# A gated recurrence with a maxout layer on one core: column quarters, a four-step weight conversion, one joined sum, and a new order of all work

## The chip, the cores and the metric

The kernel runs on one core of a Trainium2 chip. A core has a matrix engine (PE), a vector engine (DVE), an activation engine (ACT), a general engine (POOL) and a sequencer for transfers (SP); each works through its own queue in order, and semaphores make one wait for another. The metric is device time in microseconds; the time of a kernel is the median of its runs.

## What is computed

The first half is a recurrence with a complex gate per channel; the second is a three-way maxout layer on its output. The four weight matrices arrive as 64-bit floats, everything else as 32-bit.

```python
batch, n_heads, seq, head_dim = 4, 8, 768, 48       # x: 3072 tokens, 384 wide; d_ff 768
mag = np.sqrt(a_re * a_re + a_im * a_im)
scale = np.minimum(mag, 0.999) / (mag + 1e-06)
a = (a_re + 1j * a_im) * scale
for t in range(S):
    S_ = a[:, :, t, :, None] * S_ + k[:, :, t, :, None] * v[:, :, t, None, :]
    y[:, :, t] = np.einsum('bhd,bhde->bhe', q[:, :, t], S_.real)
x = y.transpose(0, 2, 1, 3).reshape(B * S, H * D)
h = np.maximum(np.maximum(x @ w1, x @ w2), x @ w3)
out = h @ w_out
```

(The reference keeps real and imaginary parts of the state apart; the lines are shortened here.)

## The kernel before

**Tiling.** Tokens are worked in 12 groups; a group is one stretch of 128 positions of two sequences, its two chunks named x and y. Six groups after one another belong to one pair of sequences and hand on a state.

**Order.** The order of all work is written out by hand in one string, `SCHEDULE`: some 1,900 words such as `csx:3`, a step, a chunk and a group. `program` runs them in turn, and each word issues its instructions at the end of its engine's queue (`Bound` chains the instructions of an engine in that order). Transfers go into SP's queue, accumulating transfers into POOL's. `SLOTS` says, for each matrix result in turn, which of four pairs of PSUM banks it gets. `OTHER` is a set of words whose step goes to DVE in place of ACT or POOL: `copy`, `magnitude`, `increase` and a few branches ask `other()`.

**Steps of a group**, in the order in which the data passes them:

- loads `Lr`, `Li` (gates), `Lk`, `Lq`, `Lv`; a load of k, q or v is four transfers (`load_kq`, `load_v`);
- gates, `sqr` to `turn` (function `gates`): the logarithm of the magnitude goes to the tile Ln, the angle in turns to w. Ln, Exp, Sin and Arctan run on ACT; Ln and Exp live in one activation table, Sin and Arctan in another, and `activation` issues a table load when the set changes. `relu`, `abs`, `Lnop` and `addw` are the steps that may change engines;
- angles: `cs` sums the turns along time with a triangular matrix on PE, `t` and `nf` take off whole turns, `af`, `sa` and `sb` give cosine and sine, `Cd` carries the last angle to the next group by an accumulating transfer;
- turns: `sums`, `En`, `Ek`, `Eq`, `F`, `f0` to `f3` (decay factors), `mk`, `mq`, `uk`, `uq`, `kEn` (DVE products), `tpk`, `tpq` (transposes on PE), `Kc`, `Qc` (copies out of PSUM);
- factors and scores: `Q1`, `Q2`, `KB`, `QB`, `QG` on DVE, `A` and `B` on PE, `g0` to `g3` and `b0`, `b1` pick the results;
- state: `dk` on PE, `h0` to `h3` on DVE; output of the recurrence: `y` on PE, `x` copies it out;
- the layer: `U01` to `U12` are up products of nine 128x128x256 matmuls each, `u01` to `u12` the relu and the maxima. The down product is a scheme of seven products: `S1` to `S4` on DVE, `P1` to `P7`, `Px`, `Py` on PE, and `r1`, `r6`, `r5`, `r7`, `r57`, `ox`, `oy` add the parts into the output tile `ot`; `D` stores it. Group 0 uses a plain form (`U01x` and so on, `O`, `o`) while the weights are not yet there.

**Weights.** Twelve blocks are loaded raw (`WL0` to `WL11`, 768 KB each) and converted from 64 to 32 bits by integer steps on the two words of a number: `Wa` on ACT (absolute value of the high word, scaled), then `Wb` (clamp), `Wc` (shift), `We` (merge the low word's top bits) and `Wf` (merge the sign) on DVE. `Wg` subtracts one weight block from another, `T`, `t`, `M` and `m` build a product of w1 and w_out, `J1` to `J4` the seven products' factors.

**Buffers.** Some tiles are fixed (`const`), others come from pools with one or two buffers under a tag; chunk tiles such as `t`, `nf`, `CS`, `K` and `Q` rotate through two. Ek and Eq share a tag.

Of the kernel before, what the change touches and what calls it, by code (L numbers as in the profile page):

```python
# [26 lines left out]
turn1:0 Lry:1 sqr:1 t1:0 WL11:0 Lkx:0 tx:0 nfx:0 Wa11:0 Wb10:0 csy:0 afx:0 sax:0 mkx:0 Wb11:0 Wc10:0 Lix:1 sbx:0
uqx:0 sqi:1 Lix:2 Wc11:0 Lky:0 tpqx:0 ty:0 add:1 f3x:0 f2x:0 ukx:0 Fy:0 Qcx:0 We10:0 Wf10:0 nfy:0 tpkx:0 We11:0
lnL:1 WL2:0 Q2x:0 kEnx:0 Eqy:0 expe:1 Eky:0 relu:1 xor:1 expw:1 QBx:0 Kcx:0 abs:1 T2:0 T0:0 t0:0 CL:0 KBx:0 WL1:0
Wa1:0 pw:1 Q1x:0 mky:0 Wb1:0 f0y:0 f1y:0 Wc1:0 t2:0 f2y:0 Wf11:0 lne:1 Lnop:1 Ax:0 g0x:0 Lry:2 g1x:0 We1:0 g2x:0  # L30
half:1 Lqy:0 Cdx:0 f3y:0 Liy:2 Lvx:0 mqy:0 Wa2:0 Wb2:0 lnw:1 expL:1 M0:0 mulw:1 Wc2:0 M1:0 mulai:1 dkx:0 Wf1:0
stt:1 afy:0 say:0 sby:0 Wg1:0 sqi:2 WL4:0 Wa4:0 g3x:0 sumsx:1 Lrx:2 Cdy:0 sqr:2 M2:0 We2:0 QGx:0 atan:1 Wb4:0 Wf2:0
Lvy:0 Eqx:1 Enx:1 Ekx:1 uky:0 Zg:0 tpky:0 h1x:0 m0:0 m1:0 Lkx:2 Z3:0 Wg2:0 Wc4:0 uqy:0 tpqy:0 Lqx:1 Kcy:0 Qcy:0
Bx:0 b0x:0 turn:1 b1x:0 h2x:0 mqx:1 Fx:1 f0x:1 We4:0 f1x:1 Wf4:0 f2x:1 add:2 csx:1 tx:1 yx:0 KBy:0 Q2y:0 nfx:1 xx:0
h3x:0 f3x:1 lnL:2 expe:2 Q1y:0 WL5:0 Wa5:0 Lkx:1 sumsy:1 csy:1 Eky:1 ty:1 Ay:0 kEny:0 Wb5:0 WL7:0 relu:2 mkx:1
g0y:0 Wc5:0 expw:2 U01x:0 nfy:1 abs:2 u01x:0 Lvy:1 We5:0 Eqy:1 Z2:0 g1y:0 Wa7:0 QBy:0 afy:1 Wf5:0 Eny:1 g2y:0 g3y:0
Wb7:0 Wg4:0 U11x:0 xor:2 By:0 dky:0 U02x:0 Lvx:1 b1y:0 h1y:0 b0y:0 QGy:0 yy:0 addw:2 lnw:2 expL:2 xy:0 U11y:0 Wg5:0
u02x:0 U02y:0 afx:1 half:2 u11x:0 Wc7:0 lne:2 We7:0 mulw:2 mulai:2 sbx:1 h2y:0 Z4:0 sax:1 h3y:0 stt:2 atan:2 Wf7:0
U12x:0 u12x:0 say:1 sby:1 Cdy:1 WL8:0 Cdx:1 turn:2 ukx:1 uqx:1 U01y:0 u01y:0 u11y:0 Wa8:0 U12y:0 csy:2 ty:2 u12y:0
csx:2 tpqx:1 tx:2 u02y:0 Qcx:1 nfy:2 Lnop:2 nfx:2 tpkx:1 Fy:1 kEnx:1 Wb8:0 Wc8:0 We8:0 Kcx:1 Wg7:0 Wf8:0 U21y:0  # L40
Wg8:0 KBx:1 f0y:1 u21y:0 Lky:1 Lqy:1 mky:1 afy:2 sumsx:2 dkx:1 Q1x:1 f1y:1 f2y:1 f3y:1 Enx:2 U21x:0 u21x:0 afx:2
U22y:0 u22y:0 Oy:0 Lqx:2 mqy:1 uky:1 uqy:1 tpqy:1 Ekx:2 Lix:3 Q2x:1 say:2 sby:2 sbx:2 sax:2 Eqx:2 h0x:1 h1x:1 QGx:1
h2x:1 oy:0 QBx:1 mkx:2 h3x:1 Qcy:1 Q1y:1 tpky:1 Kcy:1 Ax:1 g0x:1 Q2y:1 Liy:3 sqi:3 Fx:2 sumsy:2 g1x:1 g2x:1 U22x:0
Lrx:3 u22x:0 g3x:1 f3x:2 f2x:2 f1x:2 f0x:2 Lry:3 sqr:3 add:3 lnL:3 expe:3 Ay:1 relu:3 J3:0 g0y:1 g1y:1 mqx:2 g2y:1
Bx:1 KBy:1 kEny:1 lne:3 Ox:0 Eky:2 b1x:1 Eny:2 QBy:1 b0x:1 h0y:1 ukx:2 By:1 Eqy:2 yx:1 g3y:1 xx:1 b1y:1 Lqy:2 mqy:2
Lvx:2 ox:0 Lky:2 mky:2 b0y:1 tpkx:2 expw:3 Kcx:2 uqx:2 Lnop:3 uqy:2 tpqx:2 Qcx:2 QGy:1 dky:1 h1y:1 kEnx:2 sumsx:3
uky:2 Ekx:3 h2y:1 Eqx:3 Enx:3 yy:1 xy:1 Fy:2 f3y:2 h3y:1 dkx:2 f2y:2 abs:3 KBx:2 h0x:2 h1x:2 Q1x:2 f0y:2 f1y:2
U11:1 u11:1 tpky:2 Kcy:2 Lky:3 QBx:2 QGx:2 addw:3 Lqx:3 h2x:2 mqx:3 h3x:2 xor:3 half:3 Cdx:2 tpqy:2 Qcy:2 Q2x:2
lnw:3 kEny:2 expL:3 sumsy:3 Eqy:3 Q2y:2 Eny:3 Lkx:3 mkx:3 Fx:3 Eky:3 U01:1 Ax:2 Q1y:2 J1:0 mulw:3 mulai:3 g0x:2
g1x:2 u01:1 Cdy:2 f3x:3 f2x:3 g2x:2 g3x:2 J2:0 Bx:2 f0x:3 Dx:0 f1x:3 Dy:0 stt:3 KBy:2 h0x:3 U12:1 b0x:2 b1x:2 u12:1  # L50
S3:1 Lvy:2 yx:2 U02:1 QBy:2 Lvx:3 Lry:4 atan:3 turn:3 Liy:4 csy:3 csx:3 Lix:4 Lrx:4 sqr:4 sqi:4 add:4 lnL:4 ty:3
xx:2 By:2 u02:1 Ay:2 S1:1 nfy:3 relu:4 tx:3 expe:4 S2:1 expw:4 P5:1 P6:1 g0y:2 afy:3 say:3 sby:3 nfx:3 sbx:3 g1y:2
afx:3 sax:3 abs:4 dky:2 P1:1 Lqy:3 g2y:2 g3y:2 b1y:2 J4:0 QGy:2 P7:1 Px:1 P2:1 b0y:2 h0y:2 h1y:2 ukx:3 tpkx:3 lne:4
Lnop:4 r1:1 Liy:5 mky:3 h2y:2 h3y:2 S4:1 Kcx:3 uqx:3 yy:2 Lqx:4 kEnx:3 mqy:3 tpqx:3 Qcx:3 P3:1 r6:1 xy:2 Py:1 r5:1
r7:1 P4:1 Fy:3 uky:3 r57:1 f0y:3 f1y:3 xor:4 half:4 oy:1 ox:1 Q1x:3 addw:4 dkx:3 h1x:3 Lvy:3 f2y:3 f3y:3 h0y:3
h2x:3 sumsx:4 Ekx:4 h3x:3 lnw:4 QGx:3 expL:4 Eqx:4 Fx:4 KBx:3 U11:2 Dx:1 QBx:3 mulai:4 Q2x:3 f2x:4 Enx:4 u11:2
# [986 lines left out]
```

## Time and profile before

| what | us |
|---|---|
| runs | 557.14, 561.46, 561.69 |
| median | 561.46 |
| span of the profiled execution | 556.9 |
| the same: PE / DVE / ACT / POOL busy | 524.6 / 490.4 / 370.0 / 74.4 |
| time in activation table loads (45) | 57.7 |
| time in the 792 matmul records of the up products | 177.4 |

The span runs from the first to the last instruction of one execution. Busy time is the union of an engine's instructions; for PE their ends are modelled, so a busy PE is not yet one at its peak. One matmul in 32-bit floats is two records. Nearly every instruction carries line 210, the helper that records all of them, so groups are told apart by the names of the tiles they write and read: `xhx<-xhx,up` is the running maximum, `ot<-ot,op` the joining of the down product, `xhx<-xhx` and `w<-w,xhx` weight steps, `g<-g,f` the state's decay.

### The profile page before, as it was taken

To read this page: it belongs to the slowest core of one execution; us is meant where nothing else is said; L and a number is where in the kernel's file an instruction comes from. 1 tells how busy PE (TensorE), PEld (TensorE's weight loads), DVE (VectorE), ACT (ScalarE), POOL (GpSimd) and SP (SyncE) were. 2 spreads that over 40 slices of the span, in tenths; PEclk is the share of its full clock that TensorE was granted. 3 is DMA by queue.
4 is the path that set the end of the run, shared out by engine and by line. 5 is a ranking of instruction groups with operands and counts; after the bars stand their busy time and mean duration, and the time that the engine had idled before them with its cause. 6 is when DMAs were issued, how large, how long until landed. Compare 5 with 4: busy or idle time off the path is not lost.

```text
span 556.9 us, 22739 instructions
## 1 busy us (share of the span) xinstructions
PE 524.6 (94%) x10086; PEld 449.0 (81%) x10086; DVE 490.4 (88%) x770; ACT 370.0 (66%) x652; POOL 74.4 (13%) x117
## 2 busy tenths in 40 slices
PE   1669799989999999999999999999999999999997
PEld 0356588778888898888988888988888888998986
DVE  5999999989998899999988897999999999886524
ACT  5999989867965867787766858777646855530100
POOL 8105250002030001000120200120010020000000
PEclk9869999999999999999999999999999999999999
DMA  8977976456055164235364136542361144000000
GB/s 218 287 191 156 206 154 102 78 105 123 18 108 109 21 123 77 48 63 92 68 115 82 33 61 121 110 88 50 58 126 31 32 88 82 10 31 2 7 25 29
DMA packets 142530, 49.09 MB, mean 88 GB/s; under 512 B 130528, under 2 KB 135648, under 8 KB 142432
## 3 DMA queue, kind: packets, MB, share of 16 engines
q1 hardware_dynamic: 136272, 37.77, 31.9%
q0 software_dynamic: 6160, 9.87, 10.4%
q8 instruction: 79, 1.29, 1.0%
q14 instruction: 19, 0.16, 0.1%
HBM read 33.03 MB, written 4.72 MB: 68 GB/s over the span
## 4 chain that ended last, share of the span: by engine, by line
PE 84%; DVE 6%; DMA 4%; SPq 2%; issue 1%; ACT 1%; POOL 0%; DVEq 0%
PE up L210 34%; PE op L210 24%; PE y L210 7%; PE A L210 5%; PE tp L210 4%; PE dk L210 4%; PE sums L210 3%; PE cs L210 2%; SPq L210 2%; DMA xhx<-in_moe_w_out_dram 2%; PE F L210 2%; DVE xhx L210 1%; PE B L210 1%; DMA k<-in_k_dram 1%; DMA ar<-nf 1%
## 5 line engine op out<-in xcount | busy, mean ns | idle before, releaser
L210 PE MATMUL up<-xhx,w 128*128 128x256 f32 x792 | 177.4, 382 | 0.1
L210 PEld LDWEIGHTS up<-xhx,w 128*128 128x128 f32 x792 | 148.6, 190 | 21.5 <-PE B L210 0.3
L210 ACT ACT_TABLE_LOAD x45 | 57.7, 1283 | 1.5 <-PEq L1027 0.8
L210 ACT COPY atm<-B 32x128 f32<-32x128 f32 x96 | 24.5, 255 | 36.9 <-DVE atm L210 22.9
L210 PE MATMUL op<-wo,xhx 128*128 128x192 f32 (+1 forms) x220 | 48.5, 364 | 0.0
L210 DVE TENSOR_TENSOR Q<-Q,f 112x1024 f32<-112x1024 f32 (+1 forms) x48 | 45.4, 950 | 0.8 <-ACT Q L210 0.6
L210 ACT ACTIVATE f<-F 48x232 f32<-48x232 f32 x96 | 34.4, 359 | 13.2 <-PE F L210 5.4
L210 POOL DMA_DIRECT2D ar<-nf x40 | 34.2, 1280 | 65.3 <-DVE ar L210 54.7
L210 PE MATMUL y<-atm,vb 128*32 128x64 f32 x1152 | 39.4, 221 | 1.4 <-issue 1.1
L210 PEld LDWEIGHTS op<-wo,xhx 128*128 128x128 f32 x220 | 36.5, 190 | 4.3 <-DVE q L210 0.3
L210 POOL DMA_DIRECT2D Ln<-e x11 | 11.1, 1005 | 214.6 <-ACT e L210 53.9
L210 PE MATMUL y<-QG,g 112*32 112x64 f32 x1408 | 38.4, 219 | 0.9 <-issue 0.8
L210 PEld LDWEIGHTS y<-atm,vb 128*32 128x32 f32 x1152 | 32.5, 109 | 6.4 <-issue 3.6
L210 PEld LDWEIGHTS y<-QG,g 112*32 112x32 f32 x1408 | 34.8, 109 | 1.3 <-issue 1.0
L210 DVE TENSOR_TENSOR ot<-ot,op 128x192 f32<-128x192 f32 (+1 forms) x67 | 27.1, 413 | 9.0 <-PE op L210 4.3
L210 PE MATMUL op<-wo,strassen 128*128 128x192 f32 x176 | 33.0, 331 | 0.0
L210 PE MATMUL A<-Q,K 112*32 112x80 f32 x1536 | 31.6, 234 | 1.3 <-DVE Q L210 1.3
L210 DVE COPY_PREDICATED atm<-masko,A 128x256 f32<-128x256 uint8 x72 | 31.2, 435 | 1.6
L210 PE MATMUL op<-w,strassen 128*128 128x192 f32 x176 | 32.5, 329 | 0.0
L210 PEld LDWEIGHTS A<-Q,K 112*32 112x32 f32 x1536 | 27.2, 110 | 5.0 <-issue 1.9
L210 ACT COPY Q<-tp 112x1024 f32<-112x1024 f32 x23 | 23.3, 1013 | 10.3 <-PE tp L210 10.0
L210 ACT COPY ot<-op 128x192 f32<-128x192 f32 (+1 forms) x13 | 4.5, 342 | 38.2 <-PE op L210 38.2
(151 smaller groups left out, 1120.8 us busy)
## 6 DMA issues: line engine op xcount, KB each, us to landing
ar<-in_a_re_dram SPq DMA_DIRECT2D x24, 192.0 KB, 3.7
ai<-in_a_im_dram SPq DMA_DIRECT2D x24, 192.0 KB, 3.8
q<-in_q_dram SPq DMA_DIRECT2D x96, 48.0 KB, 2.6
k<-in_k_dram SPq DMA_DIRECT2D x96, 48.0 KB, 2.9
vb<-in_v_dram SPq DMA_DIRECT2D x96, 48.0 KB, 3.1
out_dram<-ot SPq DMA_DIRECT2D x23, 192.0 KB, 2.8
Ln<-e POOLq DMA_DIRECT2D x11, 384.0 KB, 4.7
w<-L POOLq DMA_DIRECT2D x9, 384.0 KB, 4.7
```

The costliest lines, as they stand in the source:

```text
L210: ins = f(*a, **kw)
```

## The change

Five things change together.

1. `cs` is computed in four column quarters of the PE array, 32 wide, in place of two halves of 64: eight matmuls of 192 columns in place of four.
2. The weights' conversion has four steps in place of five. `Wb` now comes first and clamps the high word from both sides, `Wa` is a Prelu with a slope that keeps the sign and the scale, `Wc` shifts, `We` merges the low word and writes the result. `Wf` is gone.
3. `r5` and `r7` become one addition, `r75`, over two neighbouring half tiles.
4. Three biases of activations are numbers in the instruction in place of a column in memory. The tiles of k, q, t, nf, CS, Ln, Ek, Eq, En, K, Q and ot are fixed pairs in place of pool tiles; Ek and Eq have their own.
5. `SCHEDULE`, `SLOTS` and `OTHER` are new from end to end. The loads stand in bundles, once a group; the words of one kind for x and y stand together more often; 52 words are in `OTHER` in place of 38.

The diff, without the three lists:

```diff
-    LAST = float(np.array(0x0FEFFFFF, dtype=np.int32).view(np.float32))
+    LAST = float(np.array(0x47EFFFFF, dtype=np.int32).view(np.float32))
...
-        if step == "a":
-            activation(out=ex.bitcast(FP), in_=high.bitcast(FP), func=AF.Abs, scale=2.0 ** -112)
-        elif step == "b":
-            dve.tensor_single_scalar(out=ex.bitcast(FP), in_=ex.bitcast(FP), scalar=LAST, op=OP.min)
+        if step == "b":
+            dve.tensor_scalar(out=ex.bitcast(FP), in0=high.bitcast(FP), scalar1=LAST, scalar2=-LAST, op0=OP.min,
+                              op1=OP.max)
+        elif step == "a":
+            activation(out=ex.bitcast(FP), in_=ex.bitcast(FP), func=AF.Prelu, alpha=-2.0 ** 32,
+                       scale=-2.0 ** -112 if i in (0, 3, 6) else 2.0 ** -112)
         elif step == "c":
-            if i in (0, 3, 6):
-                dve.tensor_scalar(out=ex, in0=ex, scalar1=3, scalar2=-0x80000000, op0=OP.logical_shift_left,
-                                  op1=OP.bitwise_or)
-            else:
-                dve.tensor_single_scalar(out=ex, in_=ex, scalar=3, op=OP.logical_shift_left)
+            dve.tensor_single_scalar(out=ex, in_=ex, scalar=3, op=OP.logical_shift_left)
         elif step == "e":
-            dve.scalar_tensor_tensor(out=ex, in0=low, scalar=29, in1=ex, op0=OP.logical_shift_right, op1=OP.bitwise_or)
-        elif step == "f":
-            dve.scalar_tensor_tensor(out=dst.bitcast(I32), in0=high, scalar=-0x80000000, in1=ex,
-                                     op0=OP.bitwise_and, op1=OP.bitwise_xor)
+            dve.scalar_tensor_tensor(out=dst.bitcast(I32), in0=low, scalar=29, in1=ex, op0=OP.logical_shift_right,
+                                     op1=OP.bitwise_or)
...
-                activation(out=e, in_=e, func=AF.Ln, scale=1e-6 * math.exp(-LNMAX), bias=least)
+                activation(out=e, in_=e, func=AF.Ln, scale=1e-6 * math.exp(-LNMAX), bias=math.exp(-LNMAX))
...
-                for j in range(2):
-                    dst, m = ps[j * L64:(j + 1) * L64, ch * HC:(ch + 1) * HC], slice(ch * L64, (ch + 1) * L64)
-                    mm(out=dst, lhsT=upto[:, m], rhs=every(T["w", g][:, c * DM:(c + 1) * DM], j), start=True, stop=True)
+                for o in (0, L64, 32, L64 + 32):
+                    j, m = o // L64, slice(ch * L64 + o % L64, ch * L64 + o % L64 + 32)
+                    mm(out=ps[o:o + 32, ch * HC:(ch + 1) * HC], lhsT=upto[:, m],
+                       rhs=every(T["w", g][:, c * DM:(c + 1) * DM], j), start=True, stop=True)
...
-            E = T[name, x] = nat2.tile([P, DM], FP, tag=name[:1 + (n == 1)], name=name[:1 + (n == 1)])
+            E = T[name, x] = es[name][c]
...
+                if name == "r75":
+                    two_ = ot.rearrange("p c n -> p (c n)")[:, NH:3 * NH].rearrange("p (u n) -> p u n", u=2)
+                    again = yl.rearrange("p (u n) -> p u n", u=1).to_broadcast([P, 2, NH])
+                    dve.tensor_tensor(out=two_, in0=again, in1=ps[:, 1, 0:DM].rearrange("p (u n) -> p u n", u=2), op=OP.add)
+                    return
```

Where the prediction speaks of the lists, it speaks of these places. Old, around `h0x:3` and `U12:1`, and new, around `Q1y:2`:

```
old: ... stt:3 KBy:2 h0x:3 U12:1 b0x:2 b1x:2 u12:1 S3:1 Lvy:2 yx:2 U02:1 QBy:2 Lvx:3 ...
new: ... atan:3 Cdx:2 Cdy:2 turn:3 h0y:2 Q2y:2 h3x:2 Q1y:2 U01:1 U02:1 sumsx:3 b0x:2 ...
```

The head of the new list, and one of its bundles of loads:

```
Lrx:0 sqr0:0 Lix:0 sqi0:0 add0:0 lnL0:0 expe0:0 expw0:0 lne0:0 relu0:0 Lnop0:0 Zf:0 CL:0 Lry:0 WL0:0 Wb0:0 Liy:0 sqr1:0
abs0:0 sqi1:0 WL3:0 Wa0:0 add1:0 xor0:0 lnL1:0 expe1:0 expw1:0 lne1:0 relu1:0 WL6:0 Wc0:0 Wb3:0 We0:0 half0:0 Lnop1:0
...
u12:4 Lix:8 Liy:8 Lkx:6 Lvx:6 Lqx:6 Dx:3 Dy:3 Lqy:6 S3:4 h1x:5 h1y:5 Q2y:5 sumsy:6 Fx:6 lnw:7 Eky:6 Eny:6 Enx:6 afx:6
```

More of the change, by code (lines that the diff above doesn't have):

```diff
@@ L27 @@
[L27 to L56, printed above, removed]
@@ L138 @@
+xx:8 abs:10 xy:8 relu:11 xy:9 Qcx:10 addw:11 Qcy:10 u01:9 xx:10 Kcy:11 Qcy:11 xx:11 u11:11
 """.split())
@@ L546, in gates @@
             else:
[L547 removed]
+                activation(out=part("Ln") if g >= ADDS else L, in_=L, func=AF.Relu, scale=-0.5, bias=LNMAX)
         elif name == "Lnop":
```

240 lines of the change are left out of this document (131 added, 109 removed).

## The prediction

> **What bounds the kernel now.** The page comes first, for the busy shares and the slices of the span.
>
> ```profile
> span 556.9 us, 22739 instructions
> PE 524.6 (94%) x10086; PEld 449.0 (81%) x10086; DVE 490.4 (88%) x770; ACT 370.0 (66%) x652; POOL 74.4 (13%) x117
> PE   1669799989999999999999999999999999999997
> DVE  5999999989998899999988897999999999886524
> ACT  5999989867965867787766858777646855530100
> ```
>
> TensorE (PE) is full from the tenth slice on; before that VectorE (DVE) is full and PE is not. Averages hide this, so the second view is busy time by stretch (columns: length, then busy time and instructions of PE, weight load, DVE, ACT, POOL; granted clock; DMA share; GB/s).
>
> ```profile
> 0.00:14.00 14.00, 1.80 (x3) 0.69 (x4) 7.47 (x19) 7.98 (x17) 11.26 (x40) 1.00 0.83 219
> 14.00:56.00 42.00, 32.83 (x353) 20.32 (x354) 41.59 (x67) 41.48 (x69) 10.73 (x18) 0.84 0.87 209
> 56.00:84.00 28.00, 23.47 (x550) 19.92 (x550) 27.86 (x43) 24.47 (x48) 11.52 (x13) 1.00 0.84 179
> 84.00:142.00 58.00, 56.25 (x1301) 45.61 (x1300) 55.82 (x86) 45.66 (x83) 5.01 (x6) 1.00 0.57 102
> 142.00:250.00 108.00, 107.03 (x2156) 93.91 (x2155) 100.36 (x158) 80.25 (x136) 10.90 (x13) 1.00 0.37 71
> 250.00:530.00 280.00, 279.86 (x5612) 247.52 (x5611) 248.13 (x388) 169.81 (x304) 24.99 (x30) 1.00 0.34 65
> ```
>
> From 14 to 84 us DVE idles 0.41 + 0.14 = 0.55 us, from 84 to 142 us another 2.18. PE idles 1.11 us from 142 to 530 us, all of it but 0.14 before 250 us. So the time is made of two pieces: DVE work up to some place in the list, then PE work from there to the end. To find the place I summed over the schedule list, word by word, DVE work so far plus PE work still to come, at the durations of the groups (the main ones are quoted below), neighbours' overlap taken off. The largest sum stands at the word h0x:3, and the timeline shows it as the first row here, with the PE block (U12:1) and the DVE maximum (u12:1) that follow it:
>
> ```profile
> 139.01 0.55 DVE L210 TENSOR_TENSOR g<-g,f 112x384 f32<-112x384 f32 x1
> 139.48 0.95 DVE L210 TENSOR_TENSOR xhx<-xhx,up 128x768 f32<-128x768 f32 x1
> 139.63 4.15 PE L210 MATMUL up<-xhx,w 128*128 128x256 f32 x18
> 553.39 0.62 DVE L210 TENSOR_TENSOR ot<-ot,op 128x192 f32<-128x192 f32 x2 [0.56 <-PE op L210]
> ```
>
> From 139.6 us PE has 413.8 us of nearly unbroken work to 553.4; the last addition and its store take the other 3.5. What happens before 139.6 us is what the change can shorten: DVE's queue, with its 6.53 us of idle in the first 14 us (14 - 7.47).
>
> The three runs were 557.14, 561.46 and 561.69 us. The profiled execution (556.9) lies 4.6 below the median, near the fastest run. I add the change of the span to 561.46.
>
> **The change, part by part.** Weights. The twelve blocks lose step f, which merged the sign. Step b (clamp) now reads the strided high words itself and keeps the sign; ACT's step a becomes Prelu; c loses a second operation; e writes the result.
>
> ```profile
> L210 DVE SCALAR_TENSOR_TENSOR w<-w,xhx 128x768 int32<-128x768 int32 x3 | 2.9, 952 | 0.0
> L210 DVE TENSOR_SCALAR xhx<-xhx 128x768 f32<-128x768 f32 x12 | 7.5, 621 | 2.8 <-ACT xhx L210 2.7
> L210 DVE TENSOR_TENSOR w<-w,L 128x768 f32<-128x768 f32 x11 | 10.5, 951 | 0.0
> L210 DVE TENSOR_SCALAR Ln<-L 128x768 f32<-128x768 f32 x4 | 2.2, 551 | 0.0
> L210 DVE TENSOR_TENSOR k<-E,k 128x384 f32<-128x384 f32 x24 | 13.2, 550 | 0.0
> L210 DVE COPY K<-tp 112x1024 f32<-112x1024 f32 x7 | 8.6, 1222 | 1.6 <-PE tp L210 1.6
> ```
>
> Removed: 12 x 0.952 = 11.4 us of DVE. The clamp in place was 0.621 on contiguous words. The trace has no single-input row on every second word; the bounds are 0.62 (no penalty) and 0.95 (the speed of two-input rows). Step f read the same stride at 0.952, as fast as the contiguous 0.951 of w<-w,L, so the stride itself costs nothing there; I take 0.62 and keep 12 x 0.33 = +4.0 us for the range. [...] Steps c and e do not get dearer; the longer chain (DVE, ACT, DVE) adds a handover per block, with ACT's queue (the gate steps that DVE needs next) behind a Prelu that waits for DVE; DVE has other list words between, so nothing. Abs, Relu and Copy run under either table here; should Prelu need its own, that is up to 24 loads at the price below. I take none.
>
> Not all 11.4 us comes back. I compared the DVE words issued up to the binding place of each list. In the new one the largest sum stands at Q1y:2. Only the old list has, by then, twelve f, Wg8 (0.95), mqx:3, mkx:3 and h0x:3 (three of 0.55): 14.0 us. Only the new one has Lnop:3, addw:2, u12:1, add:4, turn:3 (five of 0.95), Qcx:0 (1.22), relu:1, relu:2, xx:1, h0y:2 (four of 0.55), and afy:1 and u11x:0 (about 0.4 each, smaller than any row above): 8.9-9.0 us. Several of these came from ACT and POOL through the OTHER list: freed DVE time is refilled. Difference 5.1 us. Four instructions fewer overlap less (the g row above starts 0.47 before the next but lasts 0.55, so 0.08 each): 4.8. And the old list had by its place more PE work done, sumsx:3 and Fx:3:
>
> ```profile
> 243.20 0.68 PE sums L210 x16
> 265.42 0.49 PE F L210 x32
> 267.50 1.45 PE cs L210 x16
> 271.75 1.24 PE A L210 x64
> ```
>
> 0.68 + 0.49 = 1.2 us that PE still has to do. First term: 4.8 - 1.2 = **-3.6 us**. DVE idle before the place (6.5 us at the head, 2.7 later) I leave as it is: both lists start with loads of a and the first weight block, and neither has more to do without them.
>
> Column quarters. The cs row is two chunks, 8 records each, two at a time: 0.725 us a chunk, four waves of 192 columns, 0.18 a wave. The new form has 16 records, four at a time: again four waves. A is such a form (64 records, 16 waves of 80 columns, 0.0775 each, 0.97 ns a column): 0.744 a chunk. The sums row, 16 records of 192 columns, gives 0.68. So -0.045 to +0.02 a chunk; I take -0.03, over 12 chunks after 250 us: **-0.4 us**; bounds -1.1 and +0.5 over all 24.
>
> A second ridge. In the new list the same sum at QBx:5, some 110 us of PE work further on, is only 0.3 us below that at Q1y:2; in the old list the stretch lies 7.2 below, and DVE idled 7.64 us from 142 to 250 us (108 - 100.36). Idle that was free is now on the path beyond 0.3 us. While DVE was the bound (14 to 142 us) it idled 2.73 us in 128; the same rate over 108 us is 2.3, of which 2.0 counts: **+2.0 us**, bounds 0 and +7.3.
>
> Joined sums, immediate biases, buffers.
>
> ```profile
> L210 DVE TENSOR_TENSOR ot<-ot,op 128x192 f32<-128x192 f32 x46 | 16.1, 351 | 5.9 <-ACT ot L210 3.7 <-PE op L210 1.3
> L210 DVE TENSOR_TENSOR ot<-ot,op 128x384 f32<-128x384 f32 x21 | 11.1, 549 | 3.1 <-PE op L210 3.0
> L210 ACT ACTIVATE e<-e,biases 128x768 f32<-128x768 f32 x7 | 6.6, 938 | 0.0
> L210 ACT ACTIVATE e<-e 128x768 f32<-128x768 f32 x4 | 3.4, 844 | 0.1
> L210 ACT ACT_TABLE_LOAD x45 | 57.7, 1283 | 1.5 <-PEq L1027 0.8
> ```
>
> r75 replaces 2 x 0.351 by 0.549, 11 times: 1.7 us of DVE, nearly all after the ridges under PE, so nothing; the last addition stays. A bias as an immediate saves 0.094 a time on ACT, hidden under PE later and under DVE early. Own buffers for Ek and Eq only remove waits: nothing.
>
> ACT pays for the new order: counted along the list, the sets of Exp/Ln and Sin/Arctan alternate 67 times instead of 45.
>
> ```profile
> 22.64 0.35 ACT L210 ACTIVATE f<-F 48x232 f32<-48x232 f32 x1
> 23.01 1.28 ACT L210 ACT_TABLE_LOAD   x1
> 24.31 0.52 ACT L210 ACTIVATE w<-w 128x384 f32<-128x384 f32 x1
> ```
>
> One switch costs 1.32 us here (22.99 to 24.31), so 22 x 1.32 = 29 us of ACT. Up to the first ridge it is 14 loads against 9, 6.6 us, partly paid by the words given to DVE; ACT idled 3.5 + 12.3 us from 56 to 142 us, which covers it. Without that cover those 6.6 us count. Later ACT idles 27.8 of 108 and 110 of 280 us. I take nothing. [...]
>
> Loads. SP issues in list order. Lqx:0 now stands behind 5.3 MB instead of 4.3, Lkx:0 behind about as much as before.
>
> ```profile
> 12.53 3.11 SPq L210 DMA_DIRECT2D q<-in_q_dram  x4
> 25.39 0.55 DVE L210 TENSOR_TENSOR q<-E,q 128x384 f32<-128x384 f32 x1
> 39.08 0.54 SPq L210 DMA_DIRECT2D strassen<-in_moe_w_dram  x1
> ```
>
> The DMA view gives such a load's time to landing (last column, us):
>
> ```profile
> strassen<-in_moe_w_dram SPq DMA_DIRECT2D x2, 768.0 KB, 4.9
> ```
>
> 1 MB at 209 GB/s is 4.8 us; q was issued 12.9 us ahead of its use, so it is covered. The blocks 2 and 4 are used 9 to 13 us of DVE work earlier, at about 40 us; block 4 was issued at 39.08 in the old order, behind one load of k and one of v more, some 3 us each (as the q row). So it is issued near 33 us, lands 4.9 later, near 38, and is wanted near 40: 0 to +3 us, I take 0. Steady-state loads move further from their first use in most groups; PE's idle of 0.14 us after 250 leaves nothing to gain there. POOL issues fewer accumulating transfers, and is not waited for.
>
> Sum: -3.6 - 0.4 + 2.0 = -2.0; span 554.9, time 561.46 - 2.0 = **559.5**.
>
> **Rivals.** *Slower: the table switches reach PE.* ACT feeds PE's operands (Q, K, the exponentials, the first maximum). Each of the 22 new switches that lands in a chain with no slack costs PE 1.32 us. From six of 22 on (7.9 - 2.0 = +5.9) it is slower by over 1%; half of them, 14.5 - 2.0, give 574. Against it:
>
> ```profile
> PE 84%; DVE 6%; DMA 4%; SPq 2%; issue 1%; ACT 1%; POOL 0%; DVEq 0%
> ```
>
> ACT holds 1% of the chain that ended last, with 45 loads, and idles 27.8 of 108 us from 142 to 250. For it: from 14 to 84 us ACT idles only 0.52 + 3.53 of 70 us, and two of the new loads fall there. Chance 0.16.
>
> *DVE stays the bound to 250 us.* If all 7.6 us of idle recurs, -4.0 + 7.3 = +3.3, 564.8; with the clamp at 0.95, 568.8. Chance 0.14, half of it beyond +1%.
>
> *Faster: less idle and less spread.* If the two runs 4.4 us above the fastest come from late transfers, loads and handovers placed further apart remove that: 559.5 - 4.6 = 554.9; with no idle on the second ridge 552.9. For it: the profiled execution shows the work fits 556.9. Against: no row shows what the longer runs lost. Chance 0.30.
>
> *The quarters do nothing*: 0.4 us, inside the forecast.
>
> **The numbers.** The forecast, 556 to 563, has 0.40. I count 1% (5.6 us: below 555.9, above 567.1) as what this measurement tells from no change. Faster: 0.9 of 0.30 and 0.1 of 0.40, 0.31. Slower: 0.95 of 0.16, half of 0.14 and a trace of the forecast, 0.24. The rest, 0.45, within 1%. The range 551 to 568.8 leaves out most of the switch rival (0.16) and little below; all unknown bounds lie in it except their sum.
>
> **What would show it.** Step b near 0.62 us; no f rows; DVE busy 11 us less on weights and refilled, so its total within 3 us of 490; a PE block like U12:1 reached about 4 us earlier, near 136 us; cs pairs at about 1.4 us; 67 table loads with PE idle behind ACT no longer than now; DVE idle from 142 to 250 us down from 7.6 to 2 or 3. It is wrong if b is near 0.95, if PE waits for ACT beyond 142 us, or if DVE idles for DMA around 40 us.

## The result, and the profile after

The changed kernel takes 562.96 us (median of 20 runs, 560.22 to 566.68); the kernel before took 560.16 in 20 runs of the same comparison (556.03 to 563.11). The ratio is 1.0051, 95% interval 1.0029 to 1.0074: half a per cent slower, 3.5 us above the forecast of 559.5 and inside its range. By the 1% bound nothing changed; but the interval excludes 1, and a gain of 2.0 us was forecast where 2.8 us were lost.

The profiled execution after took 564.95 us, 2.0 above its median, with a span of 563.1; the one before lies below its own median. Part of the 6.2 us between the two spans is therefore chance, and a second profile of the same kernel, `new_order_again` below, has a span of 557.0. Both are used.

The page of the kernel after, with the shares of the chain that ended last as its fifth line and the queue that brings PE's instructions as its last (packets, MB, share of time):

```profile
span 563.1 us, 23036 instructions
PE 527.1 (94%) x10278; PEld 448.2 (80%) x10278; DVE 485.0 (86%) x759; ACT 388.4 (69%) x666; POOL 70.1 (12%) x111
PE   3489689999999999999999899999899999999997
ACT  7988977987869886993848497879657935552100
...
PE 80%; DVE 9%; ACT 4%; DMA 2%; issue 2%; SPq 2%; DVEq 0%
...
q8 instruction: 81, 1.33, 1.0%
```

The same stretches as before, in the same columns:

```profile
0.00:14.00 14.00, 5.36 (x54) 2.23 (x54) 7.54 (x19) 10.77 (x23) 11.32 (x40) 1.00 0.86 266
14.00:84.00 70.00, 53.20 (x893) 38.43 (x894) 66.28 (x107) 62.20 (x106) 23.01 (x29) 0.88 0.93 200
84.00:142.00 58.00, 57.62 (x1233) 46.94 (x1235) 54.21 (x81) 48.25 (x83) 4.15 (x5) 1.00 0.41 75
142.00:250.00 108.00, 107.39 (x2311) 94.57 (x2300) 104.37 (x161) 88.40 (x145) 9.19 (x11) 1.00 0.34 66
250.00:530.00 280.00, 274.66 (x5607) 240.47 (x5609) 243.43 (x381) 177.20 (x309) 22.48 (x27) 1.00 0.30 60
```

Two things stand out. From 14 to 84 us DVE now idles 3.72 us of 70 where it idled 0.55. And from 250 to 530 us PE, which had idled 0.14 us, idles 5.34. In the second profile of the same kernel these stretches read:

```profile
14.00:84.00 70.00, 57.20 (x925) 41.77 (x924) 67.92 (x110) 63.33 (x109) 23.33 (x29) 0.95 0.93 199
142.00:250.00 108.00, 107.59 (x2168) 94.76 (x2158) 103.72 (x159) 89.16 (x144) 9.18 (x11) 1.00 0.33 64
250.00:530.00 280.00, 276.81 (x5676) 242.94 (x5675) 241.82 (x377) 173.87 (x306) 22.44 (x27) 1.00 0.30 60
```

DVE idles 2.08 us early on, and PE 3.19 late. The clock granted early is 0.95 here and 0.88 there.

The timeline of the kernel after shows the words that the prediction spoke of, and PE's waits after 250 us. In brackets stands the idle time ahead of the instruction and what ended it; "issue" means that nothing in the profile did.

```profile
48.32 0.73 DVE L201 COPY_PREDICATED atm<-maskd,A 128x512 f32<-128x512 uint8 x1 [1.46 <-PE A L201]
138.77 0.69 DVE L201 TENSOR_TENSOR Q<-Q,f 112x512 f32<-112x512 f32 x1
311.74 0.56 DVE L201 TENSOR_TENSOR q<-Eq,q 128x384 f32<-128x384 f32 x1 [2.97 <-DMA q<-in_q_dram]
353.32 1.31 PE L201 MATMUL A<-Q,K 112*32 112x80 f32 x64 [1.02 <-issue]
397.27 0.22 PE L201 MATMUL y<-atm,vb 128*32 128x64 f32 x1 [1.63 <-issue]
558.00 1.57 PE L201 MATMUL op<-w,xhx 128*128 128x192 f32 x8 [0.65 <-DVE ot L201]
```

Q1y:2, at which the new order's longest sum was to stand, ends at 139.46 us; the old order's h0x:3 ended at 139.56. Of the 4.8 us that DVE was to gain, 0.1 is there in this execution. The same words in the second profile:

```profile
135.33 0.69 DVE L201 TENSOR_TENSOR Q<-Q,f 112x512 f32<-112x512 f32 x1
305.11 0.56 DVE L201 TENSOR_TENSOR q<-Eq,q 128x384 f32<-128x384 f32 x1
346.66 1.31 PE L201 MATMUL A<-Q,K 112*32 112x80 f32 x64 [0.98 <-issue]
390.54 0.22 PE L201 MATMUL y<-atm,vb 128*32 128x64 f32 x1 [1.56 <-issue]
```

Here 3.5 us are there. The wait for q is gone, so it belongs to the first execution. The two stops of PE "for issue" recur at the same instructions, with nearly the same lengths: these belong to the program.

The conversion's rows (groups by shape: busy us, mean ns) are as forecast. Step b, the first three, now reads every second word and takes 551, 640 or 586 ns (the clamp on contiguous words took 621); there are no f rows:

```profile
L201 DVE TENSOR_SCALAR xhx<-strassen 128x768 f32<-128x768 f32 x3 | 1.7, 551 | 0.3 <-DMA strassen<-in_moe_w_dram 0.3
L201 DVE TENSOR_SCALAR xhx<-w 128x768 f32<-128x768 f32 x4 | 2.6, 640 | 0.0
L201 DVE TENSOR_SCALAR xhx<-xhx 128x768 f32<-128x768 f32 x4 | 2.3, 586 | 0.0
L201 ACT ACT_TABLE_LOAD x67 | 86.0, 1283 | 1.8 <-PEq L1028 0.8
L201 PE MATMUL cs<-w,upto 128*32 128x192 f32 x384 | 20.4, 345 | 6.4 <-DVE w L201 6.3 <-ACT wo L201 0.2
```

### The profile page after: what moved, and what is told of

Same layout as the page of the kernel before. It is cut to its first block, busy times and chain, and to the rows that moved or that the text cites. A ratio compares the mean times of both kernels' runs of the same rounds, so it can differ in the third digit from the quotient of the medians.

```text
span 563.1 us, 23036 instructions
## 1 busy us (share of the span) xinstructions
PE 527.1 (94%) x10278; PEld 448.2 (80%) x10278; DVE 485.0 (86%) x759; ACT 388.4 (69%) x666; POOL 70.1 (12%) x111
## 3 DMA queue, kind: packets, MB, share of 16 engines
q8 instruction: 81, 1.33, 1.0%
## 4 chain that ended last, share of the span: by engine, by line
PE 80%; DVE 9%; ACT 4%; DMA 2%; issue 2%; SPq 2%; DVEq 0%
PE up L201 32%; PE op L201 21%; PE y L201 7%; PE A L201 4%; PE tp L201 4%; PE dk L201 3%; PE sums L201 2%; PE cs L201 2%; SPq L201 2%; DVE atm L201 2%; PE F L201 2%; PE wm L201 1%; DVE w L201 1%; PE B L201 1%; ACT L L201 1%
## 5 line engine op out<-in xcount | busy, mean ns | idle before, releaser
L201 PE MATMUL up<-xhx,w 128*128 128x256 f32 x792 | 179.2, 383 | 0.1
L201 DVE TENSOR_TENSOR Q<-Q,f 112x512 f32<-112x512 f32 (+1 forms) x48 | 45.3, 951 | 0.4 <-ACT Q L201 0.3
L201 DVE TENSOR_TENSOR ot<-ot,op 128x384 f32<-128x384 f32 (+1 forms) x56 | 25.8, 464 | 13.8 <-PE op L201 9.6
L201 ACT ACTIVATE xhx<-up 128x768 f32<-128x768 f32 x16 | 12.9, 809 | 32.6 <-PE up L201 32.6
L201 DVE TENSOR_TENSOR xhx<-xhx,up 128x768 f32<-128x768 f32 x22 | 20.9, 952 | 10.3 <-PE up L201 10.2
L201 PEld LDWEIGHTS op<-w,strassen 128*128 128x128 f32 x176 | 28.9, 190 | 1.1 <-issue 0.3
```

Of the source, the lines that this page charges most:

```text
L201: ins = f(*a, **kw)
```

## The experiments

Fourteen kernels were measured in four sets, each set on another chip and with the kernel before among them, whose medians were 557.23, 560.42, 560.86 and 557.85 us. A ratio is to the kernel before of the same set. Two kernels are best compared within one set.

### The change taken apart

**The old lists with all the new code.** The lists of the kernel before stay, except that the words `Wf` go, `Wa` and `Wb` change places, `r5` goes and `r7` is `r75`. In the old list `Lkx:2` stands ahead of `mkx:1` and `ukx:1`; with the fixed pairs of tiles, chunk x of group 1 is then computed from the k of group 2, and the output is not the reference's.

```diff
- ... add0:0 Wa0:0 Wb0:0 Wc0:0 We0:0 Liy:0 Wf0:0 ... Py:1 r5:1 r7:1 P4:1 ...
+ ... add0:0 Wb0:0 Wa0:0 Wc0:0 We0:0 Liy:0 ... Py:1 r75:1 P4:1 ...
```

> The old lists with all of the new code (conversion in four steps, column quarters, joined sum, immediates, fixed tiles). In the list the words Wf are gone, Wa and Wb of a block have changed places, r5 is gone and r75 stands where r7 stood. Theory 1 (the code saves what it was costed at and the new order gives it back): the DVE work up to h0x:3 falls by the 12 f steps, 11.4 us, until ACT's own sum, 6.9 us below DVE's in the old list, takes over; so 4 to 7 us faster than the kernel before, 553.5 to 556.5 against 560.2. Theory 2 (the weights were not on the path, or Prelu's place behind the clamp costs what the f step saved): within 1.5 us of the kernel before. Theory 3 (one of the code's parts costs time by itself): 2 us or more slower.

Measured: 582.75 us, 1.0435 (1.0393 to 1.0477).

**The old lists with the conversion alone.** The kernel before, with the four-step conversion and the words in the order `Wb`, `Wa`, `Wc`, `We`; everything else as it was.

```diff
- ... add0:0 Wa0:0 Wb0:0 Wc0:0 We0:0 Liy:0 Wf0:0 ...
+ ... add0:0 Wb0:0 Wa0:0 Wc0:0 We0:0 Liy:0 ...
-        if step == "a":
-            activation(out=ex.bitcast(FP), in_=high.bitcast(FP), func=AF.Abs, scale=2.0 ** -112)
+        if step == "b":
+            dve.tensor_scalar(out=ex.bitcast(FP), in0=high.bitcast(FP), scalar1=LAST, scalar2=-LAST, op0=OP.min,
+                              op1=OP.max)
...
```

> The kernel before with the conversion in four steps alone (Wf gone, Wa and Wb change places in the list), all else old. If the conversion is what shortens the DVE's queue: 4 to 7 us faster than the kernel before, the same as with all of the new code to 1 us. If the quarters and the joined sum matter: this one is 1 to 2 us slower than the one with all of the new code. If handovers DVE-ACT-DVE cost: under 3 us gained, with DVE waits for ACT on the tiles xhx of more than 0.3 us a block in the first 70 us.

Measured: 568.4 us, 1.0194 (1.0155 to 1.0233): 11 us slower, with 11 us less work for DVE. Its timeline around block 2's clamp (49.82), with the decay h0x:3 at the end:

```profile
49.82 0.55 DVE L205 TENSOR_SCALAR xhx<-xhx 128x768 f32<-128x768 f32 x1
50.40 0.84 ACT L205 ACTIVATE xhx<-xhx 128x768 f32<-128x768 f32 x1 [2.91 <-DVE xhx L205]
51.27 0.81 ACT L205 ACTIVATE L<-pw 128x768 f32<-128x768 f32 x1
52.99 0.96 DVE L205 TENSOR_TENSOR w<-pw,L 128x768 f32<-128x768 f32 x1 [2.62 <-ACT L L205]
...
145.79 0.55 DVE L205 TENSOR_TENSOR g<-g,f 112x384 f32<-112x384 f32 x1
```

ACT's Prelu stands at the head of ACT's queue until DVE has clamped; the two L steps behind it start only then; and DVE's next word needs their result. Each engine waits for the other in turn. Over the window from 14 to 84 us the profile puts 9.9 us of DVE's waits down to ACT and 5.0 to PE, where before it was 0.2 us and none. The window as a whole:

```profile
14.00:84.00 70.00, 52.17 (x842) 35.70 (x843) 54.91 (x89) 59.57 (x104) 15.82 (x23) 0.83 0.82 190
```

DVE idles 15.1 us where it idled 0.55, more than the work that was saved. h0x:3 starts at 145.79 in place of 139.01, 6.8 us later, and the span is 6.7 us longer (563.6 to 556.9): all of the loss in the profile lies ahead of that word. (The profiled execution took 565.4 us, 3 below its median.)

**The same with the clamps shifted.** `Wb` up to four DVE words earlier and some of the `Wa` elsewhere among ACT's words, so that no Prelu would wait; block 2 as an example:

```diff
- ... g1x:0 We1:0 g2x:0 ... mqy:0 Wb2:0 Wa2:0 lnw:1 expL:1 M0:0 mulw:1 Wc2:0 M1:0 mulai:1 dkx:0 ...
+ ... g1x:0 Wb2:0 We1:0 g2x:0 ... mqy:0 lnw:1 expL:1 Wa2:0 M0:0 mulw:1 M1:0 mulai:1 Wc2:0 dkx:0 ...
```

> The kernel before with the conversion in four steps alone, as old_order_conversion, but each Wb placed up to four DVE words ahead of its Wa where the buffer allows, and the Wa of blocks 2, 3, 4, 5 and 10 behind the gate step of ACT that they had stood before. PE's order and its number of instructions are those of the kernel before. Theory H (the conversion's 11.4 us are lost in the old order because Prelu waits for DVE at the head of ACT's queue, and DVE's next gate step waits for ACT: DVE idles 9.7 us from 14 to 56 us in old_order_conversion against 0.4): most of that idle goes, 8 to 14 us faster than old_order_conversion and 0 to 5 us faster than the kernel before (552 to 557.5). Rival (the four-step conversion is slow wherever it stands): as old_order_conversion, ratio 1.015 or more.

Measured: 566.56 us, 1.0110 (1.0064 to 1.0155). Neither expectation came. The ratio is lower than without the shift (in another set), but the profile shows no gain: DVE idles 17.5 us from 14 to 84 us, and the span is 563.2, against 563.6. DVE's waits for ACT fell from 9.9 to 6.3 us, and those for PE rose from 5.0 to 10.1. Part of these may come from stops of PE of the kind that the next section describes: from 60 to 139 us they are 4.4 us here and 1.8 without the shift. So moving these words did not bring the saved work back, and which of the remaining waits decides isn't settled.

**The new lists with the old conversion.** `Wa` and `Wb` change places again, `Wf` stands behind `We`, and the five steps are computed as before.

```diff
- ... WL0:0 Wb0:0 Liy:0 ... WL3:0 Wa0:0 add1:0 ... Wc0:0 Wb3:0 We0:0 half0:0 ...
+ ... WL0:0 Wa0:0 Liy:0 ... WL3:0 Wb0:0 add1:0 ... Wc0:0 Wa3:0 We0:0 Wf0:0 half0:0 ...
```

> The changed kernel with the conversion in the old five steps (Wa and Wb of a block change places, Wf stands behind its We); lists else as in the changed kernel, PE's instructions the same. Theory 1 (in the new order DVE's queue sets PE's start, as the prediction has it): 11.4 us more of DVE before Q1y:2, less the clamp's new place, so 7 to 11 us slower than the changed kernel. Theory 2 (the new order is bound by PE and PSUM from 70 us on, and DVE has slack): 0 to 4 us slower.

Measured: 577.18 us, 1.0297 (1.0258 to 1.0335). In its timeline Q1y:2 is at

```profile
151.68 0.69 DVE L202 TENSOR_TENSOR Q<-Q,f 112x512 f32<-112x512 f32 x1
```

It ends at 152.37, 15.9 us later than in `new_order_filled` of the same set (the changed kernel with a few words moved, see below; 136.49), and the time is 15.7 us longer (561.49 there). So in the new order DVE's queue up to Q1y:2 sets the start of PE's unbroken work, as the prediction had it, and the short conversion is worth more here than the 11.4 us of its f steps. The two parts need each other: the short conversion alone costs 11 us, the new order with all but the short conversion 16, and the whole change 2.8.

### Quarters, and PE's stops

**The new order with `cs` in halves.**

```diff
-                for o in (0, L64, 32, L64 + 32):
-                    j, m = o // L64, slice(ch * L64 + o % L64, ch * L64 + o % L64 + 32)
-                    mm(out=ps[o:o + 32, ch * HC:(ch + 1) * HC], lhsT=upto[:, m],
-                       rhs=every(T["w", g][:, c * DM:(c + 1) * DM], j), start=True, stop=True)
+                for j in range(2):
+                    dst, m = ps[j * L64:(j + 1) * L64, ch * HC:(ch + 1) * HC], slice(ch * L64, (ch + 1) * L64)
+                    mm(out=dst, lhsT=upto[:, m], rhs=every(T["w", g][:, c * DM:(c + 1) * DM], j), start=True, stop=True)
```

> The changed kernel with the angles' sums in the old two column halves of 64. The prediction's term: quarters save 0.03 us a chunk, so 0.4 us slower than the changed kernel, bounds -0.5 to +1.1; the records of cs sum to 20.0 us as before the change, against 20.4. If the quarters cost something (16 records of 192 columns in place of 8): up to 0.5 us faster than the changed kernel.

Measured: 568.34 us, 1.0194 (1.0155 to 1.0234), 4.65 us above the quarters of the same set (`new_order_q_early`, which only has two loads moved; 563.69). But the `cs` group is busy 20.7 us in halves and 20.4 in quarters (20.0 in the halves of the kernel before), far too little for this. The difference is in stops of PE elsewhere, such as this one in its timeline:

```profile
109.48 0.35 PE L201 MATMUL y<-QG,g 112*32 112x64 f32 x9 [2.54 <-issue]
```

Where do such stops stand? I numbered all of PE's records of a trace in order (matmuls, weight loads and the sequencer's entries; 20,320 before and 20,690 after). In all sixteen traces the stops for "issue" after the first 60 us stand, nearly all of them, at a number that leaves the remainder 193 when it is divided by 256. The queue that brings PE's instructions moves packets of 16 KB, 79 of them before (1.29 MB) and 81 after (1.33 MB); 20,320 / 256 is 79.4 and 20,690 / 256 is 80.8. By these counts a packet is a block of 256 instructions, and PE stops at the seam between two blocks. Laid beside the landings of the packets, the sixteen traces have 1,224 seams after 60 us: at the 96 with a stop (of over 0.06 us) PE resumes 1.2 to 1.6 us after the packet of the same number landed, and at none of the others does it pass sooner than 1.2 us after. Most of the longer stops stand where small matmuls (`y`, `A`, `B`, `dk`, `tp`) make a block short: 57 of the 79 over 0.3 us follow a block that took under 3.3 us. But 63 blocks as short passed without a stop, their packet having landed in time; what sets the start of a packet isn't known. Halves have four matmuls fewer per chunk, so each seam lies at other work.

This can be tested without touching the work: spare matmuls at the head of PE's queue, where PE waits for data, shift all seams.

**The kernel before with 22 spare matmuls** (88 instructions of PE), and **with 64** (256 instructions, a whole block, so that the seams lie where they were):

```diff
+    spare = psum.tile([P, 2, 512], FP, tag="ps0", name="spare")
+    for _ in range(22):
+        mm(out=spare[0:32, 0, 0:L64], lhsT=vbs[0][:, 0, 0, 0:32], rhs=vbs[0][:, 0, 0, 0:L64], start=True, stop=True)
     program(SCHEDULE, 0)
```

> The kernel before with 22 spare matmuls (32 wide, 64 columns, on zeros, into a PSUM bank that is free) at the head of PE's queue, where PE idles until 10.5 us; all else old. Theory F (PE's instructions come in blocks of 256, 16 KB each, and PE stops where a block has not arrived: in all traces so far the stops inside a word stand at instruction 193 of a block): 22 matmuls are 88 instructions (each is two records and two weight loads), so every later block boundary falls 88 instructions earlier in the work, where short matmuls stand close in the old order; with 3.5 us a block the sum of stops goes from about 1 to about 26 us: 12 to 28 us slower than the kernel before. Rival (the stops inside words come from something else, DMA traffic or the clock): within 1.5 us of the kernel before, for 22 matmuls take under 2 us of idle PE.

> The kernel before with 64 spare matmuls at the head of PE's queue in place of 22: 256 instructions, one whole block. Theory F (stops at the block boundaries of PE's instructions): every later boundary stands where it stood in the kernel before, so the time is that of the kernel before to within 2 us, though almost three times as many matmuls were added as in old_order_spare22, which took 18 us more. Rival (spare matmuls cost by their number, or by holding PSUM or the clock at the start): slower than old_order_spare22, 20 us or more.

Measured: 577.79 us, 1.0333 (1.0277 to 1.0388), with 22; 561.65 us, 1.0013 (0.9978 to 1.0049), with 64. Three times the spare work costs nothing, a third of it 17 us. With 22 the window from 250 to 530 us is

```profile
250.00:530.00 280.00, 268.99 (x5284) 236.37 (x5276) 242.63 (x374) 169.99 (x302) 24.99 (x30) 1.00 0.33 65
```

so PE idles 11.0 us where it idled 0.14. Its timeline shows stops at small matmuls (`dk`, `B`) and at an up product that follows such a stretch:

```profile
123.21 0.56 PE L210 MATMUL dk<-vb,uk 64*64 64x48 f32 x23 [1.45 <-issue]
...
294.20 1.02 PE L210 MATMUL up<-xhx,w 128*128 128x256 f32 x4 [1.34 <-issue]
...
409.40 0.39 PE L210 MATMUL B<-QB,KB 112*32 112x32 f32 x21 [1.27 <-issue]
```

With 64 it is

```profile
250.00:530.00 280.00, 279.86 (x5611) 247.42 (x5610) 249.53 (x390) 170.45 (x304) 25.02 (x30) 1.00 0.34 65
```

**The new order in halves with 20 spare matmuls** (80 instructions).

```diff
...
+    for _ in range(20):
...
```

> The changed kernel with the angles' sums in halves, as new_order_halves, and 20 spare matmuls (80 instructions) at the head of PE's queue. Theory F: the stops at block boundaries fall from 14.6 to 9.6 us by the same sum over the trace of new_order_halves, so 3 to 6 us faster than new_order_halves (ratio to the kernel before 1.009 to 1.014 against 1.019), though nothing of the work is less. Rival (the halves cost 8 us by themselves): as new_order_halves, within 1.5 us.

Measured: 569.98 us, 1.0158 (1.0107 to 1.0208), and 9.1 us above the quarters of the same set (`new_order_again`, 560.84). The gain that was expected did not come: the stops only moved.

The sums of the stops at the seams, from 60 us on, go with the differences within a set:

| pair of one set | stops of the one, us (number) | of the other | difference | difference of the times |
|---|---|---|---|---|
| `old_order_spare22`, before | 17.2 (22) | 2.2 (4) | 15.1 | 17.4 |
| `old_order_spare64`, before | 2.5 (4) | 2.2 (4) | 0.4 | 0.8 |
| `old_order_new_code`, `old_order_conversion` | 15.7 (14) | 2.3 (3) | 13.3 | 14.4 |
| `new_order_halves`, `new_order_q_early` | 8.6 (8) | 3.0 (3) | 5.6 | 4.7 |
| `new_order_halves_spare20`, `new_order_again` | 9.9 (9) | 3.0 (3) | 7.0 | 9.1 |
| `new_order_head_spare8`, `new_order_head` | 5.9 (8) | 3.7 (3) | 2.2 | 2.3 |

The third row says why the old lists with all the new code are slower still than with the conversion alone: the quarters' 384 more records shift the seams of the old order into its dense stretches. The changed kernel's own stops after 60 us sum to 2.84 us in the first profile and 2.96 in the second, those of the kernel before to 2.17, of which 0.90 after 139 us.

### Switches, the wait for q, and attempts at mending

**22 more table loads**, two ahead of each `turn` word:

```diff
+        if name == "turn":
+            for s in sorted(set(SETS.values()) - {T["set"]}) + [T["set"]]:
+                act.preload_act_table_set(s)
```

> The changed kernel with two more table loads on ACT (to the other set and back) ahead of each turn word: 24 or more loads, 31 us of ACT. The prediction's rival (table switches reach PE, 1.32 us for each that lands in a chain with no slack): half of them would make it 14 us slower; all that lie in the first 84 us (3 groups, 8 loads, 10 us) may count, the others not by the prediction. So 0 to 3 us slower if ACT has the slack that its idle time shows from 142 us on, and some 10 us or more if the switches of the new order are what it loses.

Measured: 572.04 us, 1.0200 (1.0165 to 1.0234), 10.5 us above `new_order_filled` of the same set, so 0.48 us a load. Part of it is paid early: Q1y:2 ends at 139.26 here and at 136.49 there. The timeline shows how the price reaches PE later on:

```profile
423.29 2.57 ACT L201 ACT_TABLE_LOAD   x2
425.87 1.01 ACT L201 COPY Q<-tp 112x1024 f32<-112x1024 f32 x1
426.94 0.87 PE L201 MATMUL tp<-ident,uq 64*112 64x64 f32 x16 [2.15 <-ACT Q L201]
```

Two loads stand ahead of the copy of Q, and PE waits 2.15 us for it, although ACT idles 12.6 of the 40 us from 400 to 440. By its size this is what was expected if the switches are what the new order loses. Against it, in each of the changed kernel's own two traces only one wait of PE of over 0.15 us after 84 us is put down to ACT, of 0.19 us. Through DVE, ahead of Q1y:2, the switches may still count; the part on the prediction comes back to this.

**The load of q earlier.** In the first profile DVE waited 2.97 us for `q` at 311.74, since the new list issues `Lqx:7` directly ahead of `mqx:7`, and PE stood idle 1.68 and 0.77 us soon after. `Lkx:7` and `Lqx:7` move to behind `Lqy:7`.

```diff
- ... Lqy:7 Lry:8 sqr:8 ... P1:5 Dy:4 Lkx:7 Lqx:7 mqx:7 ...
+ ... Lqy:7 Lkx:7 Lqx:7 Lry:8 sqr:8 ... P1:5 Dy:4 mqx:7 ...
```

> The changed kernel with the words Lkx:7 and Lqx:7 moved up in the list to stand right behind Lqy:7, ahead of the loads of a for group 8 and 9 and of v for group 6 and 7; nothing else. Theory A (a load issued too late is what the new order loses after 250 us): DVE's wait of 2.97 us for q at 308.8 us goes, and with it PE's gaps of 1.68 us at 313.9 and 0.77 us at 319.7: 1.5 to 3 us faster than the changed kernel, about 560.5 against 563.0. Theory B (table switches or other handovers take it anyway, or the loads moved behind it now come late): within 0.7 us of the changed kernel, with the gaps at other places.

Measured: 563.69 us, 1.0093 (1.0059 to 1.0127). No gain that a time shows.

**The changed kernel once more**, unchanged:

> The changed kernel as it is, on this chip beside the others, for a second profile. If the wait for q at 309 us and the two gaps of PE behind it belong to the kernel, they are there again (about 3 us of DVE, 2.4 us of PE); the stops at instruction 193 of a block are again few (under 4 us in all). If they were an accident of one execution, they are gone. Ratio to the kernel before 1.003 to 1.009.

Measured: 560.84 us, 1.0020 (0.9989 to 1.0051). Its profile, shown above, has no wait for q: that wait is one execution's.

**Earlier work for PE, and the loads moved.** `Ay:0` ahead of `U01x:0`, `U11x:0` ahead of `By:0`, `Eny:1` behind `Eqy:1`, the loads as above; `SLOTS` follows.

```diff
- ... yx:0 xx:0 U01x:0 h2x:0 ... h3x:0 Ay:0 half:2 ... Wa7:0 By:0 ... We7:0 U11x:0 u11x:0 ...
+ ... yx:0 xx:0 Ay:0 U01x:0 h2x:0 ... h3x:0 half:2 ... Wa7:0 U11x:0 By:0 ... We7:0 u11x:0 ...
```

> The changed kernel with PE's idle from 57 to 72 us filled: Ay:0 ahead of U01x:0 and U11x:0 ahead of By:0, with the PSUM pairs 0 and 6 exchanged from there on, Eny:1 right behind Eqy:1 on ACT (it holds the pair that U11x:0 takes), and Lkx:7 and Lqx:7 behind Lqy:7 as in new_order_q_early. If PE's work from 70 us on sets the end in the new order (PE idles 0.5 us from 84 to 142 us in both of its profiles): the gaps of 1.88 us (yx:0 to U01x:0) and 2.4 us (U02x:0 to By:0) shrink by 2 to 3.5 us and the end with them, 557 to 559 us on a chip where the changed kernel takes 561. If DVE's queue to Q1y:2 sets it: within 1 us of the changed kernel, with PE's idle moved to 84 to 142 us.

Measured: 561.49 us, 1.0022 (0.9993 to 1.0052). The gain that was expected from filling PE's gaps is not seen.

**The same, and DVE's two waits around 40 to 50 us**: `Ax:0` between `M0:0` and `M1:0`, so that `g0x:0` need not wait for both, and `Wb4:0 Wa4:0` later, behind `Q2x:0`. Then the same with 8 spare matmuls, against the stops of 0.94 and 2.19 us that `new_order_filled` had.

```diff
- ... expL:1 Wb4:0 Wa4:0 Wa2:0 afy:0 ... Q2x:0 mulai:1 ... M0:0 M1:0 Ax:0 Fy:0 ...
+ ... expL:1 Wa2:0 afy:0 ... Q2x:0 Wb4:0 Wa4:0 mulai:1 ... M0:0 Ax:0 M1:0 Fy:0 ...
```

> new_order_filled with two of DVE's waits in the head taken away: Ax:0 stands between M0:0 and M1:0 on PE (DVE waited 0.8 to 1.5 us for it behind both), and Wb4:0, Wa4:0 stand behind Q2x:0 (DVE waited 0.3 to 0.9 us for block 4's load). If DVE's idle of 2 to 3 us from 14 to 84 us is what the new order lost against the sum: 1.5 to 2.5 us faster than new_order_filled, ratio to the kernel before 0.998 to 1.000, DVE idle from 14 to 84 us about 1. If not: 1.001 to 1.004 as before, with DVE's idle at other places.

> The same with 8 spare matmuls (32 instructions) at the head of PE's queue. Theory F: by the sum over the trace of new_order_filled with 3.2 us a block the stops fall from 6.4 to 4.3 us (they measured 3.5 where the sum gives 6.4), so 1 to 2 us faster than new_order_head, and with it about 1 to 3 us faster than the kernel before. If the stops are hidden under other waits: as new_order_head.

Measured: 563.8 us, 1.0089 (1.0051 to 1.0126), and 566.1 us, 1.0133 (1.0082 to 1.0183). Both expectations fell. The first one's DVE idles 4.5 us from 14 to 84 us, more than `new_order_filled` did (2.83): the waits moved. The second one has eight stops at the seams in place of three, 5.9 us in place of 3.7.

The new order's ratio lay between 1.002 and 1.009 over the four sets, with the kernel before at 557.2 to 557.9 us in two of them and 560.4 to 560.9 in the others. `new_order_again`, `new_order_q_early`, `new_order_filled` and `new_order_head` each belong to another set, so these ratios don't rank them; that stays open. None of the fourteen was faster than the kernel before.

## Why the prediction was off

**What held.** The frame: DVE's queue up to one word, then PE's work. `new_order_old_conversion` shows it (15.9 us at Q1y:2, 15.7 us of time). Step b costs 0.55 to 0.64 us, no f rows are left, and the loads of tables are 67, as counted. DVE's total fell by 5.4 us, against "within 3 us of 490": freed DVE time was refilled, though not quite as far.

**The first term.** "DVE idle before the place (6.5 us at the head, 2.7 later) I leave as it is" is the step that failed. DVE alone, from 14 us to the end of the binding word, in the kernel before and in the two profiles of the changed kernel (busy time and instructions, clock, DMA share, GB/s):

```profile
14.00:139.56 125.56, 122.88 (x190) 0.95 0.73 155
14.00:139.46 125.46, 118.02 (x185) 0.93 0.70 143
14.00:136.02 122.02, 117.03 (x184) 0.97 0.71 146
```

DVE's work fell by 4.9 and 5.9 us, a little more than the forecast 4.8. But its idle time, the difference of length and busy time, rose from 2.68 to 7.44 and 4.99 us (6.80 and 5.62 in `new_order_q_early` and `new_order_filled`), on average by 3.5. The head stayed, 6.46 us against 6.53. So Q1y:2 ends at 139.46, 136.02, 138.07 and 136.49, on average at 137.5, 2.1 us before the old place and not 4.8. What DVE waits for in this stretch, the kernel before first (total, times, longest):

```profile
DVE g L210 <- PE dk L210: 1.4, 2, 0.9
DVE Ln L210 <- ACT L L210: 0.2, 1, 0.2
...
DVE atm L201 <- PE A L201: 1.8, 2, 1.5
DVE hT L201 <- PE up L201: 1.4, 2, 1.1
DVE xhx L201 <- ACT xhx L201: 0.5, 1, 0.5
DVE xhx L201 <- DMA strassen<-in_moe_w_dram: 0.3, 1, 0.3
```

In all, the waits for PE went from 1.6 to 3.9 us (1.8 in the second profile), those for ACT from 0.2 to 2.1 (1.2), and there is a wait of 0.30 (1.01) us for a weight block at 39 us, which the prediction took as 0 and named as a sign of being wrong. The longest is at 48.32, where `atm` waits 1.46 us for `A`, which stands behind `M0` and `M1` in PE's queue. No single wait accounts for the loss, and the attempt to remove two of them (`new_order_head`) moved it elsewhere. The prediction also dismissed the handover, "DVE has other list words between, so nothing": in the old order with the short conversion, DVE's waits for ACT and PE took more than the conversion saves.

**PE's work left.** "From 139.6 us PE has 413.8 us of nearly unbroken work to 553.4" was true of the old order and was taken over as a sum of durations. PE's busy time from the end of the binding word to its own end, in the same three profiles:

```profile
139.56:553.36 413.80, 412.68 (x7906) 1.00 0.33 64
139.46:559.57 420.11, 413.51 (x8184) 1.00 0.30 59
136.02:553.44 417.42, 413.02 (x8184) 1.00 0.30 60
```

The work is 0.8 and 0.3 us more, where the prediction had 1.2 left over and 0.4 off for the quarters. But it has other seams: 2.8 and 3.0 us of stops after Q1y:2 against 0.9, some 2.0 us more. The timeline of before has such a stop too, which found no place in the sum:

```profile
228.81 0.24 PE L210 MATMUL y<-QG,g 112*32 112x64 f32 x1 [0.81 <-issue]
```

**The quarters.** I sized them by waves, -0.4 us. In the rows they are 20.4 us against 20.0 in the halves of the kernel before and 20.7 in those of the new order, so nothing either way. Their worth to this order, 4.7 us against halves, lies in the position of the seams and says nothing about quarters.

**The second ridge**, "+2.0 us", did not come: DVE idled 3.63 and 4.28 us from 142 to 250 us where it had idled 7.64, a little above the forecast of 2 or 3, and PE idled 0.61 and 0.41 us there, less than the 0.97 of before.

**Joined sums.** "Nearly all after the ridges under PE, so nothing; the last addition stays" missed the last group: `ox:11` now needs `r75:11`, and with it P7, so no product is left to stand between `ox:11` and PE's last one. That one waits 0.65 us for `ox:11` (at 558.00), and as long in the second profile.

**Loads.** "PE's idle of 0.14 us after 250 leaves nothing to gain there" overlooked that there was something to lose: one execution of two lost 2.46 us of PE to a late q.

The span of each profiled execution against the one of before, with measured terms alone:

| term, us | first profile | second |
|---|---|---|
| end of Q1y:2 against 139.56 | -0.10 | -3.54 |
| PE's busy time after it | +0.84 | +0.34 |
| stops at the seams after it | +1.94 | +2.06 |
| wait of PE's last product | +0.65 | +0.65 |
| wait for q | +2.46 | 0 |
| PE's other waits, each under 0.4 | +0.41 | +0.57 |
| sum, and the span | +6.2 | +0.1 |

The spans of the four profiles (these two, `new_order_q_early` and `new_order_filled`), the wait for q taken off, are on average 2.2 us above that of before. The times were 2.8 us longer in the first comparison and 0.4 in the second set. The forecast was -2.0.

**A reading.** The prediction set the span of the profiled execution, 556.9, beside the times of runs and found it 4.6 us below their median. A time is some 1.8 us above its span here (564.95 and 563.1 in the profile after, 558.73 and 557.0 in the second), so that execution took some 558.7 us and lay 2.8 below. The forecast does not hang on it, but the rival of less spread was priced by it.

**The rivals.** DVE did not stay the bound to 250 us; less spread did not come. The table switches reach PE directly in one wait of 0.19 us; but 15 loads instead of 10 lie ahead of the binding word, and 1.0 to 1.9 us more of DVE's waits there are for ACT. A new order with fewer switches was not tried, so what part of these the switches have stays open. What decided was on no list: the seams between blocks of instructions, and an order in which DVE waits some 3.5 us more.

## What to carry to other kernels

A shorter chain is worth its saved work only in an order that was made for it (here it cost 11 us in the old order, and the new order without it cost 16): check for each step that changes its engine who now waits at the head of which queue, and what stands behind it. And when a list of small matmuls is reordered, or only lengthened ahead of them, the seams between instruction blocks can move the time by some us either way (by 0.4 to 15 us in the pairs above); before a small difference is put down to an edit, run the same work with the seams shifted and with them shifted by a whole block.
